# Attention and MoE on one core: virtual times of the early parts placed anew, and a weight-sum selector of 128 columns

## The chip, the cores and the metric

The kernel runs on one core of a Trainium2 chip. The metric is the device time of one execution in microseconds, and the comparison is between medians of several runs. Engines are called as in the profile: PE is TensorE, DVE VectorE, ACT ScalarE, POOL GpSimd, SP the engine that issues nearly all DMAs here.

## The reference, cut to what matters

Two stages. A linear attention over 8 batches of 8 heads (576 rows, head size 64) with a feature map of 128 random features, then a two-layer feed-forward block ("MoE") with 512 → 2048 → 512 over all 4608 rows.

```python
def phi(x):
    proj = np.einsum('bhsd,df->bhsf', x, w_phi)
    proj = proj - np.max(np.abs(proj), axis=-1, keepdims=True)
    return np.concatenate([np.exp(proj), np.exp(-proj)], axis=-1)
q_p, k_p = (phi(q), phi(k))
kv = np.einsum('bhsf,bhsd->bhfd', k_p, v)
z = np.sum(k_p, axis=2)
num = np.einsum('bhsf,bhfd->bhsd', q_p, kv)
den = np.einsum('bhsf,bhf->bhs', q_p, z)[..., None] + 1e-06
x = (num / den)            # heads side by side: 4608 x 512
h = x @ w_in
g = h * (1.0 / (1.0 + np.exp(-1.702 * h)))
return g @ w_out
```

The two MoE weights arrive as 8-byte floats, and the kernel turns them into pairs of 16-bit values itself.

## The kernel before, in words

No instruction is written where it stands in the code. A recorder (`R`) collects all of them with their data, and a planner (`schedule`) then writes them out in one order per engine. It is a list scheduler: each engine takes, among the operations that its cost model (`cost`) calls ready, the one with the lowest priority number. That number is a virtual time: `R.part(v0, v1, first)` opens a part, and its operations get times spread from `v0` to `v1`; the engines named in `first` take the part ahead of everything else. MoE chunks run from virtual time 0 to 12 (384 rows to a unit); what must come before them has negative times. On the chip each engine then runs its list strictly in order.

The parts, by their names in the code:

- Attention units, 32 of them (`attn_unit`, one for each batch and pair of heads), at `v_att(i)`: units 0 to 3 (batch 0) far ahead, units 4 to 7 (batch 1) from `V1`, the others at an even step from 0.825. Units 0 to 5 take a path that DVE and PE handle in 32 bits, the rest one in 16-bit pieces with DMA transposes. Unit tiles: `kq`, `vn` (inputs), `sm` and `t` (row maxima and shifted projections, on DVE), `e`, `eh`, `el` (features), `kf` and `kzs` (key sums), `xf` (result), `x` (the rows for the MoE, in three buffers).
- Weights in two halves (`WV`). `load_weights` brings a block of 128x512 8-byte values by DMA, into the weight buffer itself or into a free `x` buffer as a stage. POOL, ACT and DVE (twice) rebuild 32-bit values into `wbuf`. PE sums absolute values for a scale: four matmuls for each block with the selector `pick` as the stationary matrix, whose one column of ones sends the sum to one row of `wsum`. When PE has read a stage, the next block can be loaded into it.
- `weight_scales` turns the sums into scales (`sc`, then `wg`, `sw`, `usc`, `osf`), by a small matmul with `ones`, and `split_weights` makes the two 16-bit parts of every block, ACT the upper (`wbuf<-wbuf,sw`) and DVE the lower.
- MoE chunks (`moe_chunk`): PE makes `hb` from `x` and the first weights (a chunk's j-th step), ACT and DVE make `th`, `g`, `gh` and `gl`, and PE adds `gh` and `gl` times the second weights into `ab`. The first chunks run over half the weights, so that they can begin before the second half is there.

DVE's order thus holds weight rebuilding, splits, attention and `g`/`gl` of the MoE in one list, and PE's order the sums, the attention matmuls and the MoE.

Of the kernel before, what the change touches and what calls it, by code (L numbers as in the profile page):

```python
# [20 lines left out]
P = 128  # L21
# [68 lines left out]
class _Op:  # L90
    __slots__ = (
        "eng", "meth", "args", "kw", "cost", "deps", "left", "outs", "allocs", "uses",
        "prio", "load", "passes", "end", "est", "also", "start",
    )


_READY = {"tensor": 282.5, "scalar": 240.0, "vector": 305.0, "gpsimd": 300.0, "sync": 100.0}


# [11 lines left out]
class Recorder:  # L111
# [7 lines left out]
    def part(self, v0, v1, first=()):  # L119
# [2 lines left out]
        self.groups.append((v0, v1, first, self.group))  # L122
        self.first = first

    def tile(self, buf, whole=False):
        tl = _Tile(buf, whole)
        return V(tl, (), buf.aps[0])


    def record(self, eng, meth, args, kw, also):  # L130
        o = _Op()
        o.eng, o.meth, o.args, o.kw = eng, meth, args, kw
# [59 lines left out]
    def cost(eng, meth, args, kw):  # L192
# [9 lines left out]
        if eng == "tensor":  # L202

            wide = mybir.dt.size(ap[1].dtype) == 4
            load = ap[1].shape[-1] / (1.2 if wide else 4.6)
            if meth == "transpose":
                return (load, max(n, 32) / 2.4 * (2 if n > 64 else 1) + 1.5, 1)
            if ap[2].dtype == F32:
                m = 1.3 if n < 200 else 1.0
                return (m * load, m * n / 1.2, 2)  # L210
            return (load, n / 2.4 + (14.0 if wide else 3.0), 1)
        src = ap[1] if len(ap) > 1 and hasattr(ap[1], "space") else out
        psum = "PSUM" in str(src.space)
        if eng == "scalar":
# [18 lines left out]
            return 100 + 2.2 * n  # L233
        return 400.0


    def schedule(self):
        n = 0
# [15 lines left out]
        pipe, turn, port = 0.0, 0.0, 0.0  # L254
        cand = {e: [] for e in free}
        order = []

# [17 lines left out]
        while todo:  # L275
            best = None
            for e, c in cand.items():
                t = free[e]
                pick = None
                for o in c:  # L280
                    s = max(t, o.est, turn + o.load) if e == "tensor" else max(t, o.est)
                    ok = True
                    for tl in o.allocs:
                        b = tl.buf
                        if b.ordered and b.head != tl.turn:
                            ok = False
                            break
                        av = [a for a, w in zip(b.avail, b.owner) if w is None]
                        if not av:
                            ok = False  # L290
                            break
                        s = max(s, min(av) + 175.0) if b.head >= len(b.aps) else s
# [22 lines left out]
            if o.meth.startswith("dma"):  # L315
                free[o.eng] = s + (600.0 if o.eng == "sync" else 800.0)
                pipe = max(pipe, s) + o.cost
                o.end = pipe + 1800.0
            elif o.eng == "tensor":
                turn = s  # L320
                for _ in range(o.passes - 1):
                    turn = max(turn + o.cost, turn + o.load)
                o.end = free["tensor"] = turn + o.cost
            else:
                o.end = free[o.eng] = s + o.cost
# [15 lines left out]
    def emit(self):  # L341
        g = lambda a: a.get() if isinstance(a, V) else a
        self.order = self.schedule()
        for o in self.order:
            f = getattr(getattr(self.nc, o.eng), o.meth)
            f(*[g(a) for a in o.args], **{k: g(a) for k, a in o.kw.items()})  # L346


@with_exitstack
def attn_moe_kernel(ctx, tc, q, k, v, w_phi, w_in, w_out, out):  # L350
# [73 lines left out]
    nc.vector.tensor_copy(ii[0:D], ident[0:D, 0:D])  # L424
    nc.vector.tensor_copy(ii[D:P], ident[D:P, D:P])

    ones = cp.tile([16, P], F32, name="ones")
    nc.gpsimd.memset(ones, 1.0)

    wst = static("wst", [P, NF], F32)  # L430
# [29 lines left out]
        "p (b t n) -> p b t n", t=2, n=DM  # L460
    )

    def pow2(dst, src):
# [3 lines left out]
        R.vector.tensor_scalar(dst, dst, 2.0**-50, None, ALU.max)  # L467


    NS = NJ // NH + 1  # L470
    pick = cp.tile([P, 2 * NS - 1], BF16, name="pick")
    nc.gpsimd.memset(pick, 0.0)
    nc.gpsimd.memset(pick[:, NS - 1 : NS], 1.0)

    def load_weights(j, wsum, first, last):
# [4 lines left out]
        for i, src in (  # L480
# [33 lines left out]
            for c in range(NCT):  # L514
                R.tensor.matmul(
                    wsum,
                    pick[:, NS - 1 - r : 2 * NS - 1 - r],
                    z[:, c * P : (c + 1) * P],
                    start=first and i % 2 + c == 0,
                    stop=last and i % 2 == 1 and c == NCT - 1,  # L520
# [13 lines left out]
    def allmax(dst, src):  # L534

        m1, m2 = small(1, "sc"), small(1, "sc")[0:1]
        R.vector.tensor_reduce(m1, src, AX.X, ALU.max, apply_absolute_value=True)
        tp = psa()
        R.tensor.transpose(tp[0:1, 0:P], m1, ident)
        R.vector.tensor_reduce(m2, tp[0:1, 0:P], AX.X, ALU.max)  # L540
        pow2(m2, m2)
        R.tensor.matmul(tp[:, P : P + 1], ones[0:1], m2, start=True, stop=True)
        R.vector.tensor_copy(dst, tp[:, P : P + 1])

    def weight_scales(k, wsum):

        m = small(1, "sc")[0:NS]
        m2 = small(NS, "sc")[0:NS]
        R.vector.tensor_reduce(m, wsum, AX.X, ALU.max)
        pow2(m, m)  # L550
        R.vector.tensor_scalar(m2, ident[0:NS, 0:NS], m, None, ALU.mult)
        tp = psa()
# [579 lines left out]


    xs = {}
    VB = 0.5
    V1 = (-1.1375, 0.5)
    WV = ((-9.8, 0.3, -7.2), (-7.1, 0.2, -5.4))

    def v_att(i):
        if i < 4:  # L1140
            return -10.175 + i
        if i < 8:
            return V1[0] + (i - 4) * V1[1]
        return 0.825 + (i - 8) * 0.3625

    def attention(b):
        sb = b // SB
# [21 lines left out]
        for hp in range(NHP):  # L1169
# [2 lines left out]
                R.part(u, u + (0.27 if b else 0.1))  # L1172
                tail = attn_tail(b, tl, i + 3 < NEX, bank)
            w = v_att(i)
            R.part(w, w + (0.54 if b else 0.2))
            nat = attn_load(b, hp)
            attn_unit(b, hp, nat, tail, nt, x16, i < NEX, bank)

# [1 line left out]
    for part_ in range(NH):  # L1180
        js = range(part_ * NJ // NH, (part_ + 1) * NJ // NH)
        v0, dv, v1 = WV[part_]
        wsum = R.tile(ab if part_ else hb, whole=True)[0:NS, 0:P]
        for i, j in enumerate(js):
            R.part(v0 + dv * i, v0 + dv * (i + 1))
            load_weights(j, wsum, j == js[0], j == js[-1])
        R.part(v1, v1)
        weight_scales(part_, wsum)
        R.part(v1, v1 + 0.1, ("vector", "scalar"))
        for j in js:  # L1190
            split_weights(j)
    attention(1)
# [54 lines left out]
```

## Time and profile before

| | |
|---|---|
| median of 3 runs | 1099.06 us (1098.99 to 1099.33) |
| profiled execution | 1097.82 us, of which its span is 1096.0 us |
| PE busy | 1062.2 us, 97% of the span |
| DVE busy | 857.8 us, 78% |
| ACT busy | 712.2 us, 65% |
| POOL busy | 242.4 us, 22% |

The span runs from the first instruction to the last. Busy shares are means over the whole span; the stretches differ, and in the first 120 us they differ most. The profile's wait rows name the engine that waited, what it was to do, and who ended the wait.

### The profile page before, as it was taken

To read this page: it belongs to the slowest core of one execution; us is meant where nothing else is said; L and a number is where in the kernel's file an instruction comes from. 1 tells how busy PE (TensorE), PEld (TensorE's weight loads), DVE (VectorE), ACT (ScalarE), POOL (GpSimd) and SP (SyncE) were. 2 spreads that over 40 slices of the span, in tenths; PEclk is the share of its full clock that TensorE was granted. 3 is DMA by queue.
4 is the path that set the end of the run, shared out by engine and by line. 5 is a ranking of instruction groups with operands and counts; after the bars stand their busy time and mean duration, and the time that the engine had idled before them with its cause. 6 is when DMAs were issued, how large, how long until landed. Compare 5 with 4: busy or idle time off the path is not lost.

```text
span 1096.0 us, 22834 instructions
## 1 busy us (share of the span) xinstructions
PE 1062.2 (97%) x8915; PEld 733.2 (67%) x8915; DVE 857.8 (78%) x1775; ACT 712.2 (65%) x1483; POOL 242.4 (22%) x310
## 2 busy tenths in 40 slices
PE   5997999999999999999999999999999999999997
PEld 3664677778766666678766666677876666577653
DVE  5889988999989997897789987897779877422322
ACT  4576687977677776676777677685677666432423
POOL 6546201322121212221132221121123111100000
PEclk9998999999999999999999999999999999999999
DMA  8854233454243431442243433333223220000101
GB/s 273 277 185 130 76 92 84 79 107 98 61 93 92 96 89 36 81 107 57 32 102 88 109 88 55 64 97 60 49 68 68 39 59 10 11 30 1 30 1 29
DMA packets 174252, 87.80 MB, mean 80 GB/s; under 512 B 140224, under 2 KB 164928, under 8 KB 173888
## 3 DMA queue, kind: packets, MB, share of 16 engines
q1 hardware_dynamic: 174144, 86.34, 33.0%
q8 instruction: 70, 1.15, 0.5%
q14 instruction: 38, 0.31, 0.1%
HBM read 54.59 MB, written 9.44 MB: 58 GB/s over the span
## 4 chain that ended last, share of the span: by engine, by line
PE 78%; DVE 10%; ACT 4%; issue 3%; DMA 2%; POOL 1%; SPq 1%; ACTq 0%; DVEq 0%; POOLq 0%
PE ab L346 31%; PE hb L346 29%; PE at L346 19%; DMA xT<-xs 1%; DVE sm L346 1%; DVE gl L346 1%; ACT e L346 1%; DVE ks L346 1%; DVE g L346 1%; DVE t L346 1%; ACT eh L346 1%; SPq L346 1%; DVE el L346 1%; DVE elb L346 1%; DMA tl<-in_v_dram 1%
## 5 line engine op out<-in xcount | busy, mean ns | idle before, releaser
L346 PE MATMUL hb<-x,wbuf 128*128 128x192 f16 (+3 forms) x3264 | 474.9, 280 | 1.1 <-DVE g L346 1.1
L346 PE MATMUL ab<-wbuf,gh 128*128 128x512 f16 x1152 | 335.8, 380 | 0.8 <-ACT gh L346 0.6
L346 PEld LDWEIGHTS <-wbuf 128*128 128x128 f16 x3264 | 279.1, 98 | 78.0 <-issue 0.9
L346 ACT ACTIVATE th<-hb,usc 128x384 f32<-128x384 f32 (+1 forms) x208 | 116.4, 560 | 130.7 <-PE hb L346 125.0
L346 PE MATMUL ab<-wbuf,gl 128*128 128x512 f16 x576 | 192.2, 380 | 1.3 <-DVE gl L346 1.1
L346 DVE SCALAR_TENSOR_TENSOR g<-th,hb 128x384 f32<-128x384 f32 (+1 forms) x208 | 107.6, 517 | 89.8 <-ACT th L346 87.5
L346 PEld LDWEIGHTS <-gh 128*128 128x128 f16 x1152 | 107.3, 98 | 80.4 <-ACT gh L346 2.9
L346 ACT ACTIVATE gh<-g,al 128x384 f16<-128x384 f32 (+1 forms) x176 | 107.6, 611 | 62.7 <-DVE g L346 62.4
L346 DVE SCALAR_TENSOR_TENSOR gl<-g,al,gh 128x384 f16<-128x384 f32 (+1 forms) x176 | 110.9, 630 | 39.2 <-ACT gh L346 32.9
L346 POOL TENSOR_TENSOR xf<-nf,rc 128x512 f32<-128x512 f32 x28 | 32.8, 1171 | 459.4 <-DVE rc L346 395.1
L346 PE MATMUL at<-ph,xT 128*128 128x128 f16 x944 | 108.6, 221 | 0.4 <-ACT x L346 0.4
L346 ACT ACTIVATE e<-at 128x512 f32<-128x512 f32 x144 | 85.6, 602 | 30.3 <-PE at L346 28.5
L346 DVE TENSOR_REDUCE sm<-at 128x4 f32<-128x512 f32 x126 | 86.1, 683 | 21.3 <-PE at L346 21.1
L346 ACT ACTIVATE e<-t 128x512 f32<-128x512 f32 x144 | 89.9, 640 | 9.8 <-DVE t L346 8.6
L346 PEld LDWEIGHTS <-gl 128*128 128x128 f16 x576 | 55.1, 98 | 51.1 <-DVE gl L346 7.2
L346 DVE SCALAR_TENSOR_TENSOR t<-at,ks,sm 128x512 f32<-128x512 f32 x118 | 87.5, 744 | 1.0
L346 DVE TENSOR_TENSOR el<-e,eh 128x512 f16<-128x512 f32 (+1 forms) x106 | 74.7, 704 | 12.7 <-ACT eh L346 11.1
L346 PE MATMUL at<-vs,eh 128*128 128x132 f32 x208 | 80.2, 386 | 0.0
L346 DVE TENSOR_TENSOR elb<-e,eh 128x512 bf16<-128x512 f32 x104 | 74.8, 719 | 6.7 <-ACT eh L346 6.5
L346 PEld LDWEIGHTS <-xT 128*128 128x128 f16 x944 | 70.2, 98 | 14.3 <-issue 1.3
L346 PE MATMUL at<-kzs,eh 128*128 128x132 f32 x216 | 78.2, 375 | 0.0
L346 ACT ACTIVATE eh<-t 128x512 fp32r<-128x512 f32 x105 | 66.4, 648 | 0.3 <-DVE t L346 0.2
(205 smaller groups left out, 1896.4 us busy)
## 6 DMA issues: line engine op xcount, KB each, us to landing
vn<-in_v_dram SPq DMA_DIRECT2D x64, 128.0 KB, 2.9
kq<-in_k_dram SPq DMA_DIRECT2D x32, 256.0 KB, 3.2
kq<-in_q_dram SPq DMA_DIRECT2D x32, 256.0 KB, 3.0
tl<-in_v_dram SPq DMA_DIRECT2D x18, 384.0 KB, 3.2
x<-in_moe_w_in_dram SPq DMA_DIRECT2D x10, 512.0 KB, 5.3
x<-in_moe_w_out_dram SPq DMA_DIRECT2D x10, 512.0 KB, 4.8
out_dram<-osb SPq DMA_DIRECT2D x38, 128.0 KB, 2.4
out_dram<-osb SPq DMA_DIRECT2D x16, 256.0 KB, 2.5
```

The source lines that it names most:

```text
L346: f(*[g(a) for a in o.args], **{k: g(a) for k, a in o.kw.items()})
```

## The change

Four edits. The selector `pick` hands PE a stationary matrix of 128 columns in place of 9, and the sums a tile of 128 partitions, of which 9 are read. The small matmuls of the scales take 16-bit operands (`ones`, and the powers of two), so they run in one pass instead of two. The planner's model of PE gets a price for a change between stationary sizes, a floor for narrow stationary matrices and 8 ns more for 32-bit ones. And all virtual times are set anew: the half-weights, their scales and splits, and the attention units. A function for paired matmuls is added that nothing calls.

```diff
+_SWITCH = 200.0
...
+            if ap[1].shape[-1] <= 64 and not wide:
+                return (105.0, max(105.0, n / 2.4), 1)
...
-            return (load, n / 2.4 + (14.0 if wide else 3.0), 1)
+            return (load, n / 2.4 + (22.0 if wide else 3.0), 1)
...
+                md = (self.mode(o, 0), self.mode(o, 1))
+                if md != mode:
+                    s += 95.0
+                mode = md
...
-    ones = cp.tile([16, P], F32, name="ones")
+    ones = cp.tile([16, P], BF16, name="ones")
...
-    pick = cp.tile([P, 2 * NS - 1], BF16, name="pick")
+    pick = cp.tile([P, NS - 1 + P], BF16, name="pick")
...
-                    pick[:, NS - 1 - r : 2 * NS - 1 - r],
+                    pick[:, NS - 1 - r : NS - 1 - r + P],
...
-    VB = 0.5
-    V1 = (-1.1375, 0.5)
-    WV = ((-9.8, 0.3, -7.2), (-7.1, 0.2, -5.4))
+    VB = 0.19
+    V1 = (-0.883, 0.446)
+    WV = ((-9.8, 0.364, -8.194), (-6.785, 0.2, -5.4))
+
+    SV = ((0.053, 0.1), (0.086, 0.057))
...
-            return -10.175 + i
+            return -10.175 + 0.998 * i
...
-        return 0.825 + (i - 8) * 0.3625
+        return 0.685 + (i - 8) * 0.377
...
-            R.part(w, w + (0.54 if b else 0.2))
+            R.part(w, w + (0.388 if b else 0.2))
...
-        wsum = R.tile(ab if part_ else hb, whole=True)[0:NS, 0:P]
+        wsum = R.tile(ab if part_ else hb, whole=True)[:, 0:P]
...
-        R.part(v1, v1 + 0.1, ("vector", "scalar"))
+        v2 = v1 + SV[part_][0]
+        R.part(v2, v2 + SV[part_][1], ("vector", "scalar") if part_ else ())
```

Two places show how the orders move. The first is DVE at the end of the first half of the weights, where `wg`, `sw`, `usc` and `osf` are the scales, `sm`, `t`, `kzs` and `xf` belong to attention units 1 to 3, and `wbuf<-wbuf,sw` is a split. Before, the scales stand here:

```order
L346 TENSOR_REDUCE wg_173<-at_61 128x1
L346 COPY wg_173<-at_61 128x1
L346 TENSOR_REDUCE sm_125<-ab_67 128x4
L346 RECIPROCAL sw_174<-wg_173 128x2
L346 TENSOR_TENSOR pg_175<-wg_173 128x1
L346 TENSOR_SCALAR sw_174<-sw_174 128x2
L346 TENSOR_SCALAR usc_180<-wg_173,vg_183 128x1
L346 TENSOR_SCALAR osf_182<-pg_175,vg_183 128x1
L346 TENSOR_TENSOR kzs_105<-kf_106,kzs_105 128x4x66
L346 TENSOR_TENSOR t_91<-ab_67,sm_125 128x512
L346 TENSOR_TENSOR x_112<-at_63,x_112 128x512
L346 SCALAR_TENSOR_TENSOR wbuf_169<-wbuf_169,sw_174 128x512
```

In the changed kernel the same scales stand in DVE's list so:

```order
L390 TENSOR_SCALAR sc_135<-ident,sc_134 9x9
L390 TENSOR_REDUCE sm_131<-ab_67 128x4
L390 TENSOR_TENSOR kzs_105<-kf_106,kzs_105 128x4x66
L390 TENSOR_REDUCE wg_173<-at_61 128x1
L390 COPY wg_173<-at_61 128x1
L390 TENSOR_TENSOR t_90<-ab_67,sm_131 128x512
L390 RECIPROCAL sw_174<-wg_173 128x2
L390 TENSOR_TENSOR pg_175<-wg_173 128x1
L390 TENSOR_SCALAR sw_174<-sw_174 128x2
L390 TENSOR_SCALAR usc_180<-wg_173,vg_183 128x1
L390 TENSOR_SCALAR osf_182<-pg_175,vg_183 128x1
L390 SCALAR_TENSOR_TENSOR wbuf_169<-wbuf_169 128x512 x2
```

The scales move twelve places forward, from position 111 to position 99 of DVE's list, and the first split from 122 to 108, ahead of the `xf` of attention unit 2. Between the last preparation of the sums (`sc<-ident,sc`) and the scales' first use of PE's answer (`wg`) two instructions are left, where there were ten.

The second place is PE just ahead of the first MoE products. `x_113` and `x_114` are weight stages that PE sums, `zt` and `xf` the last rows of batch 0, `xT` and `kq` belong to batch 1, and `hb<-x` is the MoE. Before (a line of dots leaves out repetitions):

```order
L346 MATMUL at_62<-ident,xf_104 128x128 x4
L346 LDWEIGHTS pick
L346 MATMUL ab_68<-x_113,pick 9x128
...
L346 MATMUL ab_68<-x_114,pick 9x128
L346 LDWEIGHTS xT_74
L346 MATMUL at_61<-ph_166,xT_74 128x128
...
L346 MATMUL at_63<-ident,kq_69 128x128 x4
L346 LDWEIGHTS wbuf_169
L346 MATMUL hb_65<-x_112,wbuf_169 128x256
```

And in the changed kernel:

```order
L390 MATMUL at_63<-ident,xf_104 128x128 x4
L390 LDWEIGHTS pick
L390 MATMUL ab_66<-x_113,pick 128x128
...
L390 LDWEIGHTS zt_190
L390 MATMUL at_62<-ii,zt_190 128x64
...
L390 LDWEIGHTS wbuf_169
L390 MATMUL hb_65<-x_112,wbuf_169 128x256
...
L390 LDWEIGHTS xT_74
L390 MATMUL at_61<-ph_166,xT_74 128x128
```

The MoE's first products now stand ahead of the projections of batch 1 (`xT`) and interleave with the sums of the weight stages, where before all of those came first.

## Rows read from the trace of the kernel before

**Rows 1.** Page, part 1: busy us (share of span) xinstructions.
```profile
PE 1062.2 (97%) x8915; PEld 733.2 (67%) x8915; DVE 857.8 (78%) x1775; ACT 712.2 (65%) x1483; POOL 242.4 (22%) x310
```

**Rows 2.** Windows: length, busy us by engine, PE clock, DMA share.
```profile
0.00:25.00 25.00, 12.68 (x48) 9.14 (x48) 11.97 (x27) 11.30 (x21) 15.53 (x34) 1.00 0.82 273
25.00:118.20 93.20, 83.51 (x519) 56.97 (x518) 84.93 (x155) 62.42 (x124) 50.36 (x35) 0.93 0.66 200
118.20:232.00 113.80, 113.50 (x916) 81.81 (x915) 106.03 (x243) 87.73 (x194) 23.10 (x32) 1.00 0.35 83
232.00:1076.00 844.00, 838.84 (x7369) 578.67 (x7367) 650.23 (x1345) 544.22 (x1137) 153.41 (x211) 1.00 0.29 62
```

**Rows 3.** Window 102.5 to 112.5 us, same columns.
```profile
102.50:112.50 10.00, 6.31 (x48) 4.82 (x47) 10.00 (x14) 5.93 (x11) 8.40 (x7) 0.50 0.60 163
```

**Rows 4.** DVE's waits, 25 to 118.2 us: total, times, longest.
```profile
DVE sm L346 <- PE ab L346: 3.5, 3, 3.1
DVE wbuf L346 <- POOL wbuf L346: 2.3, 1, 2.3
DVE sc L346 <- PE at L346: 0.7, 1, 0.7
```

**Rows 5.** DVE's waits, 118.2 to 232 us.
```profile
DVE wbuf L346 <- ACT wbuf L346: 2.4, 4, 1.3
...
DVE sc L346 <- PE ab L346: 0.9, 1, 0.9
```

**Rows 6.** Timeline of PE around two runs of weight sums: start, us.
```profile
28.02 0.28 PE L346 MATMUL at<-ekth,vts 128*66 128x128 f32 x2
28.14 0.22 PE L346 MATMUL at<-ektl,vts 128*66 128x128 f32 x1
28.29 1.20 PE L346 MATMUL hb<-wbuf,pick 128*9 128x128 bf16 x9
29.42 1.13 PE L346 MATMUL ab<-wb,t 128*128 128x256 f32 x4
...
30.71 0.62 PE L346 MATMUL hb<-wbuf,pick 128*9 128x128 bf16 x4
31.26 0.33 PE L346 MATMUL ab<-ident,kq 128*128 128x128 f32 x1
```

**Rows 7.** Timeline of PE: eleven 16-bit matmuls with 128-column stationary matrices.
```profile
338.18 0.78 PE L346 MATMUL at<-ph,xT 128*128 128x128 f16 x11
338.79 0.38 PE L346 MATMUL ab<-wbuf,gh 128*128 128x512 f16 x1
```

**Rows 8.** Groups by shape: weight loads, busy us, mean ns.
```profile
L346 PEld LDWEIGHTS <-wbuf 128*128 128x128 f16 x3264 | 279.1, 98 | 78.0 <-issue 0.9
...
L346 PEld LDWEIGHTS <-pick 128*9 128x9 bf16 x128 | 11.2, 99 | 8.2 <-issue 6.8
```

**Rows 9.** Groups by shape: DVE instructions that change sides, mean ns.
```profile
L346 DVE SCALAR_TENSOR_TENSOR t<-at,ks,sm 128x512 f32<-128x512 f32 x118 | 87.5, 744 | 1.0
L346 DVE TENSOR_REDUCE sm<-at 128x4 f32<-128x512 f32 x126 | 86.1, 683 | 21.3 <-PE at L346 21.1
...
L346 DVE SCALAR_TENSOR_TENSOR wbuf<-wbuf,sw 128x512 f16<-128x512 f32 x32 | 25.1, 785 | 3.2 <-ACT wbuf L346 2.9
```

**Rows 10.** Timeline of DVE: its first and its 27th `gl`.
```profile
117.14 0.41 DVE L346 SCALAR_TENSOR_TENSOR gl<-g,gh 128x256 f16<-128x256 f32 x1
...
231.78 0.50 DVE L346 SCALAR_TENSOR_TENSOR gl<-g,gh 128x256 f16<-128x256 f32 x1
```

**Rows 11.** Timeline of PE: use of the first and of the 27th `gl`.
```profile
118.23 0.59 PE L346 MATMUL ab<-wbuf,gl 128*128 128x512 f16 x2
...
231.04 1.25 PE L346 MATMUL hb<-x,wbuf 128*128 128x256 f16 x10
232.13 1.03 PE L346 MATMUL ab<-wbuf,gh 128*128 128x512 f16 x4
...
233.78 0.60 PE L346 MATMUL ab<-wbuf,gl 128*128 128x512 f16 x2
```

More of the change, by code (lines that the diff above doesn't have):

```diff
@@ L92 @@
         "eng", "meth", "args", "kw", "cost", "deps", "left", "outs", "allocs", "uses",
-        "prio", "load", "passes", "end", "est", "also", "start",
+        "prio", "load", "passes", "end", "est", "also", "start", "calls",
     )
+_SWITCH = 200.0
 _READY = {"tensor": 282.5, "scalar": 240.0, "vector": 305.0, "gpsimd": 300.0, "sync": 100.0}
@@ L123, in part, with pairs @@
         self.first = first
+    def pairs(self, mm, also=()):
+        o = _Op()
+        o.eng, o.meth, o.args, o.kw, o.calls = "tensor", "matmul", (), {}, mm
+        c = [self.cost("tensor", "matmul", a, k) for a, k in mm]
+        o.load, o.cost, o.passes = c[0][0], _SWITCH + sum(x[1] * x[2] for x in c) / 2, 1
+        o.deps, o.outs, o.allocs, o.uses = {}, [], [], []
+        o.end, o.est = None, 0.0
+        for a, _ in mm:
+            for i in (1, 2):
+                if isinstance(a[i], V):
+                    self.touch(o, a[i], False)
+        for a, _ in mm:
+            self.touch(o, a[0], True)
+        for a in also:
+            self.claim(o, a.tl)
+        o.left = len(o.deps)
+        for d in o.deps:
+            d.outs.append(o)
+        self.group.append(o)
+        o.prio = o.eng in self.first
+        self.ops.append(o)
     def tile(self, buf, whole=False):
@@ L131, in record @@
         o = _Op()
-        o.eng, o.meth, o.args, o.kw = eng, meth, args, kw
+        o.eng, o.meth, o.args, o.kw, o.calls = eng, meth, args, kw, None
         c = self.cost(eng, meth, args, kw)
@@ L234, in cost, with mode @@
         return 400.0
+    @staticmethod
+    def mode(o, i):
+        if o.calls:
+            return o.calls
+        st = o.args[1].t if isinstance(o.args[1], V) else o.args[1]
+        n = st.shape[-1] if i else st.shape[0]
+        return 32 if n <= 32 else 64 if n <= 64 else 128
     def schedule(self):
@@ L253, in schedule @@
         free = {e: 0.0 for e in ("tensor", "scalar", "vector", "gpsimd", "sync")}
-        pipe, turn, port = 0.0, 0.0, 0.0
+        pipe, turn, port, mode = 0.0, 0.0, 0.0, None
         cand = {e: [] for e in free}
@@ L282, in schedule @@
                     ok = True
+                    had = {}
                     for tl in o.allocs:
                         b = tl.buf
-                        if b.ordered and b.head != tl.turn:
+                        k = had[b] = had.get(b, 0) + 1
+                        if b.ordered and not b.head <= tl.turn < b.head + len(b.aps):
                             ok = False
                             break
-                        av = [a for a, w in zip(b.avail, b.owner) if w is None]
-                        if not av:
+                        av = sorted(a for a, w in zip(b.avail, b.owner) if w is None)
+                        if len(av) < k or b.ordered and tl.turn != b.head + k - 1:
                             ok = False
                             break
-                        s = max(s, min(av) + 175.0) if b.head >= len(b.aps) else s
+                        s = max(s, av[k - 1] + 175.0) if b.head + k > len(b.aps) else s
                     if not ok:
@@ L345, in emit @@
             f = getattr(getattr(self.nc, o.eng), o.meth)
-            f(*[g(a) for a in o.args], **{k: g(a) for k, a in o.kw.items()})
+            for args, kw in o.calls or ((o.args, o.kw),):
+                f(*[g(a) for a in args], **{k: g(a) for k, a in kw.items()})
 @with_exitstack
@@ L461, in attn_moe_kernel, with pow2 @@
     )
-    def pow2(dst, src):
+    def pow2(dst, src, to=None):
         R.vector.tensor_scalar(
@@ L466, in pow2 @@
         )
-        R.vector.tensor_scalar(dst, dst, 2.0**-50, None, ALU.max)
+        R.vector.tensor_scalar(dst if to is None else to, dst, 2.0**-50, None, ALU.max)
     NS = NJ // NH + 1
-    pick = cp.tile([P, 2 * NS - 1], BF16, name="pick")
+    pick = cp.tile([P, NS - 1 + P], BF16, name="pick")
     nc.gpsimd.memset(pick, 0.0)
@@ L540, in allmax @@
         R.vector.tensor_reduce(m2, tp[0:1, 0:P], AX.X, ALU.max)
-        pow2(m2, m2)
-        R.tensor.matmul(tp[:, P : P + 1], ones[0:1], m2, start=True, stop=True)
+        mb = small(1, "sc")[0:1].bitcast(BF16)[:, 0:1]
+        pow2(m2, m2, mb)
+        R.tensor.matmul(tp[:, P : P + 1], ones[0:1], mb, start=True, stop=True)
         R.vector.tensor_copy(dst, tp[:, P : P + 1])
@@ L547, in weight_scales @@
         m = small(1, "sc")[0:NS]
-        m2 = small(NS, "sc")[0:NS]
-        R.vector.tensor_reduce(m, wsum, AX.X, ALU.max)
+        m2 = small(NS, "sc")[0:NS].bitcast(BF16)[:, 0:NS]
+        R.vector.tensor_reduce(m, wsum[0:NS], AX.X, ALU.max)
         pow2(m, m)
```

## The prediction

> **What bounds the kernel now.** I read the page's busy times first, then the windows, then DVE's waits. The page gives PE 1062.2 us of a span of 1096.0 us and DVE 857.8 [rows 1], and the reader should see that PE is the bound of the whole, but not that it is so everywhere. The windows show where the 34 us of idle PE lie [rows 2]: 12.3 in the first 25 us (inputs arrive), 9.7 from 25 to 118.2 us, 0.3 from there to 232, 5.2 from 232 to 1076, and the rest in the tail, whose order the change leaves alone. From 25 to 118.2 us DVE is busy 84.93 of 93.20 us, more than PE. In the worst of it, 102.5 to 112.5 us, DVE is busy 10.00 of 10 us while PE has 6.31 at a granted clock of 0.50, its lower level of 1.2 GHz [rows 3]. So up to the first MoE products DVE sets the pace, and behind them PE does. The first `gl` leaves DVE at 117.14 us and PE uses it at 118.23 [rows 10, 11]; the 27th starts on DVE at 231.78, and PE takes it 2 us later, because PE is the one with work queued.
>
> DVE idles 8.3 us from 25 to 118.2 and 7.8 us from 118.2 to 232 [rows 2]. In the first stretch PE ended 4.2 us of it (3.5 for projections, 0.7 for a scale) and a late weight stage 2.3 [rows 4]. In the second PE ended only 0.9 us; the largest of the others are waits for ACT's splits, 2.4 us [rows 5].
>
> **The weight sums.** All 128 matmuls of `pick` remain, and become cheaper. Nine take 1.13 us from their first start to the next instruction, four take 0.55 [rows 6]: 0.116 us for each further one, and about 0.09 left over at the end of a run. A like 0.09 stands at its beginning: the matmul ahead of the run takes 0.15 us where its neighbours take 0.06. The order has 23 runs, so the sums cost 128 x 0.116 + 23 x 0.18 = 19.0 us of PE. The nearest row for what replaces them is a stream of 16-bit matmuls of 128 columns on 128-column stationary matrices: eleven in 0.61 us, 0.055 each [rows 7]. That makes 7.0 us. **PE saves 12.0 us**, 10.3 of it (112 matmuls, 19 runs) ahead of the first `gl`, 1.7 behind it.
>
> A rule speaks against this. The weight load of 128 columns could be the longer one; but the row of loads has 99 ns for 9 columns and 98 ns for 128 [rows 8], so width does not show. The Trainium skill (TensorE: Matmul & The Clock Gate, section on LDWEIGHTS) makes a load's time the number of columns over 1.2, which is 107 ns for 128 columns; spaced by that, the sums would cost 13.7 us, and the saving would be an estimated 5.3. It also says (TensorEngine Tiling (Array Packing), Restrictions and Key Properties) that narrow column tiles lose the fast weight load and that a change of tiling drains the engine, which fits the 0.116 and the two 0.09. I go by the rows.
>
> The small matmuls of the scales lose a pass each, seven in all; PE's row for a whole run of such work is under half a microsecond, and I cost them at nothing in either direction. The wider zeroing of `pick` on POOL lies in the first 2 us, long before its first use.
>
> **The order.** I counted both orders up to the same two milestones. Up to the first `gl`, DVE has three splits (0.785 each) and one reduction of `v` more, and three maxima (0.683), one `t` (0.744) and two small scalings fewer [rows 9]: 2.4 us against 2.8, with a reduction against two scalings beside it, so nothing, within half a microsecond. PE has the cheaper sums and four `hb` matmuls fewer (0.109 each, from ten in 1.09 us [rows 11]). So the order does not let the MoE start before DVE has done the same work as now. Up to the 27th `gl`, DVE has nine instructions more: three `t`, one maximum, two parts of tail features and smaller ones, 5.8 us by their means, and 5.2 as DVE starts them (it starts a 0.68 us instruction 0.60 after the last). PE has 14 matmuls more there, 1.5 us. Attention units are moved ahead of the MoE on DVE, just where DVE is the tighter engine. The DMA queue has the same 399 transfers, the early ones shifted by a place or two (the second unit's inputs pass one weight block, 0.5 us of issue); I cost that at nothing, covered by inputs that arrive long before their unit, and at one weight stage's wait, 2.3 us [rows 4], if the cover is gone.
>
> The scales of the first half come twelve places earlier on DVE, with two instructions instead of ten between question and answer of PE. The new wait would stand there, with everything on DVE behind it: from 0 to the 0.7 us that such an answer cost once [rows 4]. I take 0.4, inside the idle time below.
>
> **The sum.** Let y be DVE's idle time from 25 us to the first `gl` (8.3 now) and x that up to the 27th (16.0 now). With DVE as the pace, the span becomes 1096.0 - 8.3 + y - (1.7 - 0.4) = **1086.4 + y** by the first milestone. By the 27th, DVE is there at 231.8 - 16.0 + 5.2 + x = 221.0 + x, PE at best 1.1 us behind (as at the first), 11.7 - x us ahead of its 233.8, with 1.5 us less to do: **1082.8 + x**. The later of the two holds. PE has 10 us of new slack ahead, so what DVE waited for from PE (4.2 and 0.9) should go, and half of the stage's 2.3, which hangs on PE too: y = 2.9, span 1089.3. The 6.9 us of other waits in the second stretch arose with DVE ahead of its suppliers; with DVE behind, at worst they all stay (x = 9.8, 1092.6), at best half (x = 6.3, 1089.1). I take the middle of 1089 and 1092.6, a span of 1091. The median of the runs stands 3.06 us above this span (1097.82 is the profiled execution, 1.24 under the median), so **1094.0 us**, 0.5% faster. Most of the 12 us that PE saves turn into idle PE ahead of the first products.
>
> **The rivals.**
>
> *PE stays the bound all through* (0.15). Then the whole 12.0 us come through, a span of 1084, 1087.1 us. For it: PE is 97% busy, and the waits of DVE for PE. Against it: 10.00 of 10 us of DVE [rows 3]. By the skill's load rule alone the same case would end an estimated 6.7 us later.
>
> *DVE's waits move elsewhere* (0.22): x of 11.0 to 15.4, times of 1096.9 to 1101.3, no change that can be told. For it: four short waits for ACT's splits [rows 5], and the splits are now mixed with rebuilding, each behind ACT. Against: more slack on every supplier.
>
> *Slower, by PE's clock* (0.17). PE's work from 25 to 118.2 us falls from 83.5 to some 70 us (10.3 less, and 5 of the stretch ran at half clock in half-empty time), so PE idles a quarter of the stretch. Now its clock fell once, after two idle gaps, and stayed at 0.50 over all of 102.5 to 112.5 us [rows 3], when DVE did not need PE. A fall between 40 and 97 us, where DVE lives on PE's projections, doubles 5 us of PE work in every ten; that is up to 5 us of new DVE idle time for a fall. From x = 15.4 on it is slower; one fall on top of the worst of my two cases gives 14.8, two give 1103 to 1106 us.
>
> **The numbers.** The forecast has 0.46. With the first rival faster has 0.61, no change 0.22, slower 0.17; 0.2%, or 2.2 us, is about what these runs can tell. The range from 1087 (PE as the bound) to 1102 (no idle recovered, x = 16.0) leaves out the far ends of the first and the last case; the forecast's own range is 1090 to 1097.
>
> **What would show it.** Runs of `pick` at 0.055 to 0.06 us for each matmul, with no 0.09 around them, show the saving right; 0.107 shows the load rule. DVE busy over 95% from 25 to the first `gl`, and that `gl` at 111 to 114 us, shows the pace of DVE; PE idle in 25 to 118 us should grow from 9.7 to well over 12 us. The 27th `gl` should leave DVE at 227 to 231 us. If PE is as busy as now up to the first `gl`, or the time falls under 1089 us, DVE was not the bound and the step on it is wrong. If DVE's row of waits for PE grows, or the clock falls before 97 us, the slower case holds. Idle PE behind 232 us of more than 8 us would show that the later, evenly wider steps of the attention units cost something that I set at nothing.

## The result, and the profile after

The changed kernel takes 1100.71 us, median of 20 runs (1098.54 to 1102.09), the kernel before 1099.00 us on the same chips (20 runs, 1096.39 to 1101.23). The ratio is 1.0015, 95% interval 1.0009 to 1.0022: 0.15% slower, inside the bound of 0.2% and on the other side of the forecast of 1094.0. The time lies in the range and in the case "DVE's waits move elsewhere".

First the page of the changed kernel, part 1 (against [rows 1]):

```profile
PE 1059.3 (97%) x8908; PEld 732.0 (67%) x8908; DVE 855.0 (78%) x1775; ACT 716.9 (65%) x1483; POOL 239.4 (22%) x310
```

PE's busy time fell by 2.9 us where 12.0 were forecast, and the span grew from 1096.0 to 1097.3. The windows of the same stretches as in [rows 2], same columns:

```profile
0.00:25.00 25.00, 11.41 (x41) 7.75 (x42) 12.51 (x27) 11.80 (x23) 15.59 (x34) 0.96 0.82 272
25.00:118.20 93.20, 81.82 (x528) 59.55 (x527) 88.43 (x156) 62.97 (x126) 47.80 (x34) 0.94 0.65 200
118.20:232.00 113.80, 112.61 (x924) 81.71 (x923) 107.76 (x250) 88.73 (x194) 18.62 (x30) 1.00 0.32 81
232.00:1076.00 844.00, 838.51 (x7344) 575.60 (x7342) 641.58 (x1338) 546.76 (x1132) 157.43 (x215) 1.00 0.29 62
```

DVE did become busier from 25 to 118.2 us, 88.43 us for 84.93. From 25 us to its first `gl`, the stretch of the forecast, it was busy 85.89 of 90.66 us, which is 94.7%, just under the 95% that were to show it as the pace. The windows up to the first `gl`, before and after:

```profile
25.00:117.14 92.14, 82.45 (x513) 56.38 (x512) 83.87 (x153) 61.36 (x123) 49.67 (x34) 0.93 0.66 202
```

```profile
25.00:115.66 90.66, 79.28 (x513) 58.09 (x512) 85.89 (x151) 61.18 (x123) 45.90 (x33) 0.94 0.65 200
```

PE's idle time grew in every stretch: 12.3 to 13.6 us in the first, 9.7 to 11.4 (the forecast had well over 12), 0.3 to 1.2, 5.2 to 5.5. The runs of weight sums and their weight loads, from the timeline of PE and the groups by shape (against [rows 6] and [rows 8]):

```profile
29.01 0.22 PE L390 MATMUL at<-ektl,vts 128*66 128x128 f32 x1
29.07 1.32 PE L390 MATMUL hb<-wbuf,pick 128*128 128x128 bf16 x10
30.21 0.61 PE L390 MATMUL ab<-wb,t 128*128 128x256 f32 x2
```

```profile
L390 PEld LDWEIGHTS <-pick 128*128 128x128 bf16 x128 | 13.3, 111 | 3.8 <-issue 2.9
```

Ten sums take 1.14 us from their start to the next instruction, 0.114 each, with nothing left over at the end of the run, and the matmul ahead of it takes 0.06. So the leftover of 0.09 us is gone on both sides, but a sum costs what it cost before (0.116), not 0.055. The first and the 27th `gl` on DVE (against [rows 10]):

```profile
115.66 0.41 DVE L390 SCALAR_TENSOR_TENSOR gl<-g,gh 128x256 f16<-128x256 f32 x1
...
233.38 0.83 DVE L390 SCALAR_TENSOR_TENSOR gl<-g,gh 128x256 f16<-128x256 f32 x1
```

At the first, DVE is 1.5 us earlier than before (forecast: 3 to 6), at the 27th 1.6 us later (forecast: 1 to 5 earlier). Its waits from 25 to 118.2 us (against [rows 4]: total, times, longest) show what went and what came. Before, a line that [rows 4] leaves out, and then the changed kernel:

```profile
DVE wbuf L346 <- ACT wbuf L346: 0.6, 2, 0.4
```

```profile
DVE sm L390 <- PE ab L390: 1.7, 1, 1.7
DVE wbuf L390 <- ACT wbuf L390: 1.6, 2, 1.4
...
DVE sc L390 <- PE at L390: 0.2, 1, 0.2
```

PE's share is down from 4.2 us to 1.9 and POOL's late stage is gone; waiting for ACT's rebuilding, 0.6 us before, is 1.6.

### The profile page after: what moved, and what is told of

Read it like the earlier page. It is cut to its first block, busy times and chain, and to the rows that moved or that the text cites. A ratio compares the mean times of both kernels' runs of the same rounds, so it can differ in the third digit from the quotient of the medians.

```text
span 1097.3 us, 22801 instructions
## 1 busy us (share of the span) xinstructions
PE 1059.3 (97%) x8908; PEld 732.0 (67%) x8908; DVE 855.0 (78%) x1775; ACT 716.9 (65%) x1483; POOL 239.4 (22%) x310
## 4 chain that ended last, share of the span: by engine, by line
PE 72%; DVE 17%; ACT 5%; issue 2%; DMA 2%; SPq 1%; POOL 1%; ACTq 0%; DVEq 0%
PE ab L390 28%; PE hb L390 26%; PE at L390 17%; DVE sm L390 3%; DVE t L390 2%; DVE ks L390 2%; ACT e L390 1%; DVE g L390 1%; DVE gl L390 1%; DVE wbuf L390 1%; DVE xs L390 1%; DVE el L390 1%; ACT eh L390 1%; SPq L390 1%; DVE elb L390 1%
## 5 line engine op out<-in xcount | busy, mean ns | idle before, releaser
L390 PE MATMUL hb<-x,wbuf 128*128 128x192 f16 (+3 forms) x3264 | 470.1, 279 | 0.8 <-DVE g L390 0.7
L390 PE MATMUL ab<-wbuf,gh 128*128 128x512 f16 x1152 | 339.7, 379 | 1.9 <-ACT osb L390 1.1
L390 PE MATMUL ab<-wbuf,gl 128*128 128x512 f16 x576 | 196.8, 380 | 0.9 <-DVE gl L390 0.6
L390 DVE SCALAR_TENSOR_TENSOR gl<-g,al,gh 128x384 f16<-128x384 f32 (+1 forms) x176 | 108.2, 615 | 37.7 <-ACT gh L390 31.0
L390 PE MATMUL at<-ph,xT 128*128 128x128 f16 x944 | 95.3, 220 | 0.7 <-DVE t L390 0.7
L390 ACT ACTIVATE e<-at 128x512 f32<-128x512 f32 x144 | 85.8, 602 | 15.4 <-PE at L390 13.6
L390 PEld LDWEIGHTS <-xT 128*128 128x128 f16 x944 | 67.7, 98 | 15.7 <-issue 1.0
```

The source lines that it names most:

```text
L390: f(*[g(a) for a in args], **{k: g(a) for k, a in kw.items()})
```

## The experiments

Eighteen kernels ran. All ratios are to the kernel before on the same chip, with the 95% interval; unless said otherwise, a kernel computes all of the reference.

### What sets the price of a weight sum

A kernel with nothing but rows of matmuls, each row followed by four 512-column ones:

```diff
+    z2 = two.rearrange("p (n w) -> p n w", w=2)[:, :, 1]
+    z4 = four.rearrange("p (n w) -> p n w", w=4)[:, :, 1]
...
+    for z in (near, z2, z4):
+        for st in (even, odd[:, 1 : P + 1], even[:, 0:9], odd[:, 1:10]):
+            run(48, st, z, P)
```

> Nothing of the reference is computed: the kernel only stores zeros and runs rows of 48 matmuls of 128 moving columns on one stationary matrix of 128 or 9 columns, which begins at an even or an odd element, with a moving operand whose 16-bit elements lie side by side, 4 bytes or 8 bytes apart (the weight sums read theirs 8 bytes apart). Theory A, the moving operand's stride sets the 0.112 us: side by side 0.055 us for each matmul with 128 stationary columns, 8 bytes apart 0.11, whatever the stationary matrix. Theory B, the load of 128 columns sets it: 0.11 us in all rows with 128 columns, and the stride does nothing. Theory C, the odd beginning of the stationary matrix sets it: 0.055 with the even beginning and 0.11 with the odd one. With 9 columns, all theories expect 0.11 or more.

Timeline of PE; `near`, `two` and `four` are moving operands with 2, 4 and 8 bytes from element to element, the shape behind the names is that of the stationary matrix:

```profile
25.93 1.03 PE L56 MATMUL acc<-near,even 128*128 128x512 bf16 x4
26.80 2.84 PE L54 MATMUL acc<-near,even 128*128 128x128 bf16 x48
29.48 1.03 PE L56 MATMUL acc<-near,even 128*128 128x512 bf16 x4
30.34 2.84 PE L54 MATMUL acc<-near,odd 128*128 128x128 bf16 x48
33.02 1.03 PE L56 MATMUL acc<-near,even 128*128 128x512 bf16 x4
33.98 2.85 PE L54 MATMUL acc<-near,even 128*9 128x128 bf16 x48
36.76 1.04 PE L56 MATMUL acc<-near,even 128*128 128x512 bf16 x4
37.72 2.85 PE L54 MATMUL acc<-near,odd 128*9 128x128 bf16 x48
40.50 1.04 PE L56 MATMUL acc<-near,even 128*128 128x512 bf16 x4
...
41.38 2.88 PE L54 MATMUL acc<-two,even 128*128 128x128 bf16 x48
44.10 1.02 PE L56 MATMUL acc<-near,even 128*128 128x512 bf16 x4
...
56.12 5.71 PE L54 MATMUL acc<-four,even 128*128 128x128 bf16 x48
61.64 1.04 PE L56 MATMUL acc<-near,even 128*128 128x512 bf16 x4
```

Start to next start: 48 sums in 2.68 us side by side (0.056 each), 2.72 at 4 bytes (0.057), 5.52 at 8 bytes (0.115). With 9 columns it is 2.78 for 2.68, whether the matrix begins at an even or an odd element. So theory A holds: the stride of the moving operand sets the price, and neither the load's width nor its beginning does. All theories expected 0.11 or more with 9 columns and were wrong for elements side by side, where 9 columns cost nothing more within a run: their price is 0.10 us at the end of a run (2.78 less 2.68) and 0.09 at its beginning (the four matmuls ahead take 0.96 us in place of 0.87), the two leftovers of [rows 6].

### The columns and the order, each alone

The kernel before with the 128-column selector and the one-pass scales, the planner charged as if for 9 columns, so that every engine's order is that of before; and the changed kernel with 9 columns, in its own order.

```diff
+            raw = not isinstance(args[1], V) and ap[1].dtype == BF16
...
+            load = (9 if raw else ap[1].shape[-1]) / (1.2 if wide else 4.6)
```

> The kernel before, instruction for instruction in the same order on every engine, with the 128-column selector and the one-pass scales. Theory A (the sums save 23 x 0.18 us and some 0.4 us more, 4.6 us of PE, most of it ahead of the first MoE products, where DVE sets the pace): 0.5 to 2.5 us faster than before, 1096.5 to 1098.5. Rival (PE is the pace there too): the whole 4.6 us, 1094.4. Rival (nothing of it reaches the end): 1099.

> The changed kernel, instruction for instruction in the same order, with the selector of 9 columns. Theory A (the new order itself costs time, and the columns give a part back): 0.5 to 2.5 us slower than the changed kernel, 1101.2 to 1103.2. Rival (the columns are worth the whole 4.6 us in this order, since DVE waits for PE in it): 1105.3. Rival (columns do nothing): 1100.7.

The last two kernels of the study bring the sums near the price of the forecast, in either order, by another reading of the stage. They leave out the second half of each stage, so their sums and scales are other ones, while the instructions stay the same:

```diff
-                z = raw.bitcast(BF16).rearrange("p (n w) -> p n w", w=4)[:, :, 1]
+                z = raw.bitcast(BF16)[:, 0 : 2 * DM].rearrange("p (n w) -> p n w", w=2)[:, :, 1]
```

> The changed kernel, instruction for instruction in the same order, but the weight sums read elements 4 bytes apart from the first half of the stage (the upper halves of rebuilt values and of raw ones) in place of those 8 bytes apart. The sums, and with them the powers of two that scale the weights, are other ones. By the probe a sum then takes 0.057 us in place of 0.112, nearly the price that the forecast set. Theory F (the forecast's sum was right but for this price): 0.35% to 0.55% under the kernel before, 1093 to 1095. Theory A (the price was half of the error; the new order's 0.4% stays): 7 us less PE work, of which a third to two thirds come through, 2 to 4.5 us faster than the changed kernel, between 0.25% under and 0.03% under the kernel before. Rival (PE has slack enough by now where the sums stand): as the changed kernel.

> The same in the exact order of the kernel before, with the selector of 128 columns. Theory A: 2 to 4.5 us faster than the columns alone, 0.4% to 0.65% under the kernel before. Rival (the sums are hidden by now): as the columns alone, 0.25% under.

| ratio to before | 9 columns, 8 bytes | 128 columns, 8 bytes | 128 columns, 4 bytes |
|---|---|---|---|
| order of before | 1 | 0.9975 (0.9965 to 0.9984) | 0.9953 (0.9941 to 0.9966) |
| changed order | 1.0039 (1.0026 to 1.0053) | 1.0015 (1.0009 to 1.0022) | 1.0000 (0.9991 to 1.0009) |

Read down, the changed order costs 0.39%, 0.40% and 0.47%, 4.3 to 5.2 us, whatever the sums cost. (The kernel before also has the two-pass scales, which all the others lack, so the first of the three pairs and the step to e2 hold these seven passes too.) Read across, the columns are worth 0.25% and 0.24%, 2.7 us, where theory A had at most 2.5; the reading is worth 0.22% in the old order, as theory A had it, and 0.15% in the new one, 1.6 us, under its 2 to 4.5, though the two intervals (together some 0.11% either way) don't part 1.6 from 2. Theory F falls. The page's row of busy times shows what the columns saved:

```profile
PE 1056.9 (97%) x8908; PEld 734.3 (67%) x8908; DVE 858.4 (79%) x1775; ACT 713.2 (65%) x1483; POOL 243.7 (22%) x310
```

That is the columns alone (e2), 5.3 us of PE less than before, of which half reaches the end. The old order with the 4-byte reading (e18) is the fastest of all, 1093.14 us; DVE's first `gl` with the columns alone (e2), in e18 and in e17:

```profile
114.73 0.41 DVE L349 SCALAR_TENSOR_TENSOR gl<-g,gh 128x256 f16<-128x256 f32 x1
```

```profile
113.61 0.67 DVE L349 SCALAR_TENSOR_TENSOR gl<-g,gh 128x256 f16<-128x256 f32 x1
```

```profile
115.78 0.42 DVE L390 SCALAR_TENSOR_TENSOR gl<-g,gh 128x256 f16<-128x256 f32 x1
```

In the order of before the first `gl` goes from 117.14 to 114.73 (columns) and 113.61 us (reading), since DVE waited there for PE [rows 4]. In the changed order the reading moves it from 115.66 to 115.78: DVE's waits for PE's projections were already down to 1.7 us in the changed kernel, and PE's saved time turns into idle PE. The same window of the changed order with the 4-byte reading shows it, PE busy 76.50 us for 81.82, and DVE the same:

```profile
25.00:118.20 93.20, 76.50 (x522) 54.17 (x521) 88.99 (x156) 63.93 (x127) 46.14 (x34) 0.93 0.65 199
```

### Is it the work that the order puts on DVE?

From 25 us to the 27th `gl`, DVE is busy 191.45 us with the columns alone and 197.57 in the changed kernel, with idle time of 12.5 and 10.8. That makes 4.5 us, just what the order costs. (Each is one execution; kernels with the same order up to the ninth `gl` reach it at 161.20 to 163.34 us, so such an agreement is worth some 2 us either way.) Windows of either kernel, same columns:

```profile
25.00:228.90 203.90, 192.28 (x1425) 140.83 (x1423) 191.45 (x396) 149.75 (x316) 73.53 (x66) 0.97 0.50 138
```

```profile
25.00:233.38 208.38, 195.81 (x1460) 142.38 (x1459) 197.57 (x405) 153.09 (x323) 67.72 (x64) 0.97 0.47 134
```

The sum fits, so the work was taken away:

```diff
-        return 0.685 + (i - 8) * 0.377
+        return 0.825 + (i - 8) * 0.3625
```

> The changed kernel, with the line on units 8 and later as before, 0.825 + 0.3625 (i - 8). Up to the 27th gl DVE then has as much work as in the kernel before, 5.5 us less than in the changed one; the order up to the ninth gl is that of the changed kernel. Theory A (the work placed on DVE ahead of the 27th gl ate the gain): the time falls by 2 to 5 us, to 1095.7 to 1098.7. Rival (PE is the pace there, and the work on DVE is hidden): 1100 to 1101.5.

Measured: 1.0042 (1.0029 to 1.0054), slower than the changed kernel and than either expectation. The work went as meant (193.97 us busy, the 27th `gl` at 231.28), the time did not:

```profile
25.00:231.28 206.28, 191.73 (x1410) 139.19 (x1408) 193.97 (x393) 149.25 (x314) 65.94 (x61) 0.97 0.47 134
```

So theory A falls, though its sum was right to a tenth of a microsecond: one milestone does not stand for the rest of an order. DVE reached the 27th `gl` 2.1 us earlier, but the rest of the span took 870.0 us for 863.9. Over the whole span PE was as busy as in the changed kernel, and idle for 42.3 us in place of 38.0:

```profile
PE 1059.0 (96%) x8908; PEld 733.7 (67%) x8908; DVE 861.5 (78%) x1775; ACT 715.2 (65%) x1483; POOL 234.0 (21%) x310
```

Of these 4.3 us, 2.0 lie from 25 to 118.2 us and 1.5 from 232 to 432 us.

### Which edit of the plan?

Four kernels undo one part each; `VB`, `V1`, `v_att` and the span in the first, `WV` and `SV` in the second, the three costs of PE in the third, all virtual times in the fourth.

> The changed kernel with VB, V1, v_att and the span of a unit (0.54) as before; the weights' times and the planner's costs stay changed. Its order is that of the changed kernel up to the first MoE products. Theory A (the new order costs PE in two places, 1 to 2 us ahead of the first products by the weights' times, and some 3 us behind them by the attention's times): the second part goes, 1.5 to 3 us faster than the changed kernel, 0.15% under to 0.05% over the kernel before. Rival (the times work only as a set, mixtures lose): no faster than the changed kernel, 0.15% or more over the kernel before. Rival (the weights' times cost all of it): as the changed kernel.

> The changed kernel with WV, SV and the parts of the splits as before; the attention's times and the planner's costs stay changed. Theory A: the part ahead of the first products goes, 1 to 2 us faster than the changed kernel, between 0.05% under and 0.05% over the kernel before. Rival (the times work only as a set): no faster than the changed kernel. Rival (the weights' times cost all of it): 4 us faster than the changed kernel, 0.25% under the kernel before.

> The changed kernel with the planner's costs of PE as before (no price for a change of stationary size, no floor, 14 ns for 32-bit ones), all times changed. Theory A (the times are the cause, the costs are not): within 1.5 us of the changed kernel. Rival (the costs mislead the planner): 3 to 4.5 us faster than the changed kernel, 0.15% to 0.25% under the kernel before.

> The changed kernel with all virtual times as before; only the selector, the one-pass scales and the planner's costs are changed. Theory A (all of the loss is in the new times): as the columns alone, 0.2% to 0.3% under the kernel before. Rival (the planner's costs lose it): 0.05% to 0.2% over the kernel before.

Then the costs one by one, and a mixture meant to be the best:

```diff
-                    s += 95.0
+                    s += 0.0
```

```diff
-            return (load, n / 2.4 + (22.0 if wide else 3.0), 1)
+            return (load, n / 2.4 + (14.0 if wide else 3.0), 1)
```

```diff
-                if md != mode:
+                if md != mode and s > 30000.0:
```

> The changed kernel with the planner's price of 95 ns for a change of stationary size set to 0, the 22 ns for 32-bit stationary matrices kept. In its order PE runs two projections ahead of the first products of e, as before, where the changed order lets PE wait for ACT's e with the projections behind it (2.4 us of waiting, and 1 us of projections still to do after it). Theory A (the price delays PE's plan by the first changes of size and turns this pair round, and that is most of the loss): 2 to 3.5 us faster than the changed kernel, 0.05% to 0.2% under the kernel before. Rival (the 22 ns are the cause, with their 16,000 lines of other order on PE): as the changed kernel, 0.1% to 0.2% over the kernel before.

> The changed kernel with 14 ns in place of 22 for 32-bit stationary matrices, the price of 95 ns kept. The projections stay behind the first products of e. Theory A (the price is the cause): as the changed kernel, 0.05% to 0.2% over the kernel before, with PE's wait for ACT's e of 2.4 us in its trace. Rival (the 22 ns are the cause): 2 to 3.5 us faster than the changed kernel.

> The changed kernel, where the planner counts the price of 95 ns only behind the first 30 us of its plan. All else is planned with the changed costs and times, and the two projections stand ahead of the first products of e. Theory A (the pair at the start is what the price costs): 1 to 3 us faster than the changed kernel, within 0.1% of the kernel before. Rival (the price does its harm later, spread over the order): as the changed kernel, 0.1% to 0.2% over the kernel before.

> The changed kernel with the attention's times and the planner's costs as before: only the selector, the one-pass scales and the weights' times are changed. Theory A (the costs are worth 3 us in any set of times, and the weights' times alone were worth 2.5 us under the changed costs): 0.4% to 0.5% under the kernel before, 1094 to 1095, faster than the columns alone. Rival (gains of orders don't add): 0.1% to 0.3% under it, no better than the columns alone.

| kernel (128 columns, 8 bytes) | ratio | 95% interval |
|---|---|---|
| changed | 1.0015 | 1.0009 to 1.0022 |
| attention's times as before (e5) | 0.9979 | 0.9971 to 0.9988 |
| weights' times as before (e6) | 0.9997 | 0.9988 to 1.0006 |
| costs as before (e7) | 0.9985 | 0.9976 to 0.9994 |
| all times as before (e8) | 1.0004 | 0.9995 to 1.0013 |
| no price of 95 ns (e9) | 0.9978 | 0.9970 to 0.9987 |
| 14 ns for 22 (e10) | 0.9991 | 0.9982 to 1.0000 |
| price from 30 us on (e11) | 1.0007 | 0.9999 to 1.0016 |
| attention's times and costs as before (e12) | 0.9997 | 0.9988 to 1.0006 |

Of the first four expectations, e6 came as its theory A had it (0.18% under the changed kernel), e5 gained more than theory A gave (0.36%), and e7 and e8 came nearest to the rival that blames the costs. Costs and times alone looked clean: the costs 0.30% under new times and 0.29% under old ones (e2 against e8), the times 0.10% and 0.11%. But e2 is planned for 9 columns. Against e13 below, the old plan made for 128, the old costs gain 0.11% under old times, and the old times lose 0.08% under old costs, either within the intervals. And the parts don't add. Dropping the 95 ns gains 0.37%, dropping the 8 ns 0.24%, both together (and the floor) 0.30%, though either alone was expected to gain all or nothing. Old attention times gain 0.36% with the changed costs, and nothing with the old ones (e12 is 0.12% slower than e7, inside their intervals). In the most telling run, e12, theory A (0.4% to 0.5% under) and the rival (0.1% to 0.3% under) both failed: it is as fast as before.

The trace does show one thing that the price of 95 ns does. In the changed kernel PE waits for ACT's `e` with two projections (`ab<-wb,t`) still to do:

```profile
22.46 3.40 PE L390 MATMUL at<-e,vn 128*66 128x256 f32 x8 [2.42 <-ACT e L390]
```

In the order of before these four matmuls stand ahead of `e`, where they fill the wait (columns alone, timeline of PE):

```profile
22.03 1.13 PE L349 MATMUL ab<-wb,t 128*128 128x256 f32 x4 [1.84 <-ACT t L349]
23.00 1.89 PE L349 MATMUL at<-e,vn 128*66 128x256 f32 x8
```

After the wait the granted clock stood at 0.78 from 20 to 25 us and 0.88 from 25 to 30, which made the eight matmuls 3.40 us long for 1.89. That is no trait of the order: in e3 and e17, in the same order, the clock stood at 1.00 there and the same eight took 1.94 us. And e11 put the pair back and gained 0.08%, within its interval (the clock, 0.71 from 20 to 25 us, fell there in its profile too). So the pair does not account for the loss.

### How much does a trifle do?

Two trifles in the changed kernel's price (96 and 90 ns for 95), and the old plan with 14 and 15 ns.

> The selector of 128 columns and the one-pass scales, with costs and virtual times as before, planned with the selector's true width (the columns alone were run in the exact order of before). DVE has some 120 us of work between 25 us and the ninth gl. Theory A (how much DVE has to do ahead of the ninth gl decides, and the planner's choice there turns on trifles): 0.15% to 0.35% under the kernel before. Rival (each edit of the plan has a price of its own): 0.2% to 0.3% under it as well.

> The same with 15 ns in place of 14 for 32-bit stationary matrices in the planner's costs, a trifle. The two projections still stand ahead of the first products of e, but the plan gives DVE some 12 us more work ahead of the ninth gl. Theory A: some 0.3% slower than with 14 ns, within 0.1% of the kernel before. Rival (each edit has a price of its own, and an eighth of 8 ns has next to none): as with 14 ns, 0.2% to 0.3% under the kernel before.

> The changed kernel with a price of 96 ns in place of 95 for a change of stationary size, a trifle. The plan gives DVE some 7 us more work ahead of the ninth gl than the changed kernel's. Theory A: slower than the changed kernel by 0.05% to 0.25%, 0.2% to 0.4% over the kernel before. Rival (each edit has a price of its own): as the changed kernel, 0.15% over.

> The changed kernel with a price of 90 ns in place of 95. The plan gives DVE some 2 us less work ahead of the ninth gl than the changed kernel's. Theory A: 0.05% to 0.15% faster than the changed kernel, 0 to 0.1% over the kernel before. Rival (each edit has a price of its own): as the changed kernel, 0.15% over.

| kernel | ratio | 95% interval | DVE busy, 25 us to 9th `gl` |
|---|---|---|---|
| old plan, 14 ns (e13) | 0.9993 | 0.9982 to 1.0003 | 120.25 us |
| old plan, 15 ns (e14) | 0.9981 | 0.9972 to 0.9989 | 131.39 us |
| changed, 90 ns (e16) | 1.0034 | 1.0021 to 1.0046 | 125.26 us |
| changed, 95 ns | 1.0015 | 1.0009 to 1.0022 | 128.12 us |
| changed, 96 ns (e15) | 1.0002 | 0.9993 to 1.0011 | 136.58 us |

Both theories fall. The work ahead of the ninth `gl` does not decide: with the changed plan the time falls as that work grows, against what theory A expected, with the old plan it shows nothing clear (0.12% between two intervals of 0.1% either way), and e9, with less of that work than any row here (115.93 us), is among the fastest. And an edit has no price of its own: 90, 95 and 96 ns, which mean the same to any reader of the plan, lie 0.32% apart. No part of the plan was worth more than 0.37% above. Four quite different plans (e2, e5, e9 and e14) end between 0.9975 and 0.9981. And e13 is e2 with a planner that knows the selector's true width and the one-pass scales: that alone left 0.07% of the 0.25% that e2 had gained.

## Why the prediction was wrong, point by point

**The price of the sums: the first step that failed.** The prediction took "the nearest row" for the new sums, `at<-ph,xT` at 0.055 us [rows 7], and made 12.0 us of it. That row has as many columns, but its operand lies side by side; the sums read every fourth 16-bit element (the line with `w=4` in `load_weights`). They cost 0.114. By the prediction's own form that leaves 128 x 0.002 + 23 x 0.18, some 4.4 us; the totals of PE fell by 5.3 (before to e2) and 4.0 (e3 to changed). The two 0.09 were read rightly, and e1 shows them apart.

**The rule on the load.** The weighing went by the right row for the wrong question. The pitch of the sums does not follow the width of the load: the probe has 128 columns at 0.056 us, and 9 columns as well, so the 0.116 was no loss of a narrow matrix either. (The load's own record did grow a little in the changed kernel, 111 ns for 99.) The Trainium skill (TensorE: Matmul & The Clock Gate, section on LDWEIGHTS) gave an estimated saving of 5.3 us, near to what came, but not for its reason: 0.107 and 0.115 happen to lie close. The sign that the prediction set up, "0.107 shows the load rule", would have confirmed the wrong cause; only a probe that moves stride and width apart could tell.

**The order up to the first `gl`: the second step that failed.** It was counted as "nothing, within half a microsecond" on DVE. DVE's busy time from 25 us to the first `gl` grew from 83.87 to 85.89 us, though it ran two instructions fewer there (151 for 153), and y was 4.8, not 2.9. The `gl` came at 115.66, not at 111 to 114. DVE's waits for PE fell, by 2.3 us of the 4.2 that were to go, and the stage's 2.3 went entirely; the wait for ACT's rebuilding grew by 1.0.

**The order up to the 27th `gl`.** DVE was busy 190.74 us from 25 us to the 27th `gl` before, and 197.57 in the changed kernel:

```profile
25.00:231.78 206.78, 196.79 (x1432) 138.58 (x1431) 190.74 (x396) 149.93 (x317) 73.24 (x66) 0.97 0.49 136
```

So the work was sized 1.6 us too small (5.2 for 6.8), and x was 10.8 for 6.3 to 9.8. With x alone the formula gives 1082.8 + 10.8 = 1093.6, with the work as well 1095.2, and 2.1 are left to the span of 1097.3. They lie behind the 27th `gl`. PE took it 1.0 us after its start, as forecast (1.1), at 234.36 us:

```profile
234.36 0.59 PE L390 MATMUL ab<-wbuf,gl 128*128 128x512 f16 x2
```

From there it needed 862.9 us to the end, where before it needed 862.2 [rows 11] and 1.5 less were forecast. So the sum closes, but e4 says that this way of counting is itself at fault: it took 3.6 us of that work off DVE, and the kernel became slower. Time won ahead of the milestone was lost behind it, which the sum held fixed.

**Had the price been right.** e17 has nearly the forecast's price, twelve sums in 0.70 us, 0.058 each:

```profile
87.76 0.86 PE L390 MATMUL ab<-wbuf,pick 128*128 128x128 bf16 x12
88.46 0.40 PE L390 MATMUL ab<-x,pick 128*128 128x128 bf16 x4
```

The forecast for that was 0.5% faster. It is as fast as before. So of the error of 0.6% the price explains 0.15%, and the rest is the order, which the three pairs put at 0.39% to 0.47% and which the prediction sized by the DVE work up to two milestones. That the time still lay in the stated range, in the case of a rival, is luck as far as the forecast's sum goes.

**The rivals.** "DVE's waits move elsewhere" named the time, at 0.22, but its x of 11.0 and more was not reached, and its splits hardly count (2.7 us for 2.4). "PE stays the bound" falls by the windows. "Slower, by PE's clock" looked at 40 to 97 us, where the clock stood at 1.00; it fell at 20 to 30 us instead, beside the fall near 100 us that the kernel before has too, and in this profile but not in that of e3, which has the same order.

**What stays open.** Why one order is 0.4% better than another. The price at PE's start (e11), the work on DVE up to the 27th `gl` (e4) and up to the ninth (e14 to e16) were each tried as the cause and refuted. The pages show where the loss lands, but not why: in each of the three pairs the changed order has PE busy for longer with the same matmuls, but for the seven passes (by 1.1, 2.4 and 2.7 us), and idle for longer as well (by 2.0, 2.5 and 3.5), in one execution of each. The rows of e3, e18 and e17, whose spans are 1099.1, 1091.1 and 1097.3 us, beside those above and [rows 1]:

```profile
PE 1063.3 (97%) x8908; PEld 728.4 (66%) x8908; DVE 855.8 (78%) x1775; ACT 715.9 (65%) x1483; POOL 238.0 (22%) x310
```

```profile
PE 1050.9 (96%) x8908; PEld 727.2 (67%) x8908; DVE 858.4 (79%) x1775; ACT 713.1 (65%) x1483; POOL 243.5 (22%) x310
```

```profile
PE 1053.6 (96%) x8908; PEld 725.8 (66%) x8908; DVE 855.2 (78%) x1775; ACT 716.0 (65%) x1483; POOL 238.4 (22%) x310
```

Which of many small waits adds up differently was not isolated.

## What to carry to other kernels

Before a row lends its price to a new instruction, compare how both operands lie in memory, not only their shapes and types; when a rule and a measured time agree, ask what else would give that time. Where a list scheduler sets the order, price a new order by running it beside the same order with the other edits undone, and change one number by a few per cent to see how much of a result is the planner's chance: here 5 ns of a 95 ns cost did 0.2%. Try a mechanical saving first in the order that was there without it: here the columns alone gave 0.25% in it, with the nearer reading 0.47%, and in the changed order neither beat the kernel before.

## What was not expected of the hardware

- A matmul of 128 moving 16-bit columns took 0.056 us with elements side by side, 0.057 at 4 bytes and 0.115 at 8 bytes, at a granted clock of 1.00. The Trainium skill (SBUF — State Buffer, Specifications (TRN2)) asks for two hits in each 16-byte line for full bandwidth, and has a penalty without a figure for each crossing to a new line; 8 bytes apart gives two hits, and the measured rate is half, so here the measurement decides.
- Nine stationary columns cost PE as much as 128 within a run (0.056), and 0.09 and 0.10 us at its two ends.
